# ConvNeXt-V2 block: channel rows on three of every four partitions, every third block stored whole, reloads issued by SP

## The chip, the core and the metric

The kernel runs on one core of one Trainium2 chip. The metric is device time in microseconds (us) of the whole kernel, taken from runs without a profile. One further execution was profiled; the views shown are of that one. TensorE is PE in the profile (its weight loads are PEld), VectorE DVE, ScalarE ACT, GpSimd POOL and SyncE SP.

## The reference

One image `x` of 512 x 512 pixels with 96 channels, bf16:

```python
out = depthwise_conv3x3(x, dw)            # zero padding
h   = layernorm(out, over the 96 channels) # no gain or bias
h   = gelu(h @ w1)                         # 96 -> 384
gx  = sqrt(sum over all pixels of h*h + 1e-6)      # one number for each of 384
nx  = gx / (mean(gx) + 1e-6)
h   = grn_gamma * (h * nx) + grn_beta + h
return x + h @ w2                          # 384 -> 96
```

The sum over all pixels (`gx`) has to be complete before the second matrix product can be finished. So the kernel goes over the image twice.

## The kernel before

The image is cut into 128 blocks of 4 rows (2048 pixels each). `BATCHES` groups them, mostly by four, for the layernorm's statistics.

**First pass.** It is a software pipeline over slots `s`, one block a slot in steady state. The dictionary `at` says which stage of which block is done in which slot. In a slot SP issues, in this order: `load_x` (the block's pixels for four slots later), `stage_read`, `stage_write`, in some slots `stage_bcast` (4 DMAs) or `stage_rows` (2 DMAs), and `store_next` (one third of a stored block). For a block, DVE transposes the pixels, PE does the convolution taps, ACT evacuates (`y_bf`), POOL or ACT squares (`ysq`), PE sums, and POOL multiplies by the inverse deviation (`stage_norm`, tile `yn`). `stage_write` sends `yn` to DRAM (`yn_dram`, 96 channel rows of 4 KB a block, in four DMAs) and one slot later `stage_read` fetches it, channels on partitions, into one of six `ynT` tiles (`yn_ring`). Two slots after that PE multiplies it by the centred `w1p`, and ACT applies the gelu.

A block is four quads of 512 pixels. `cm_quads(b)` says how many quads come out with hidden channels on partitions (DVE then does three `bn_stats` of each); the rest come out with pixels on partitions, and PE sums their squares (`gram_next`). All four quads of a whole block (`is_whole`) are channel-major, and its gelu output goes to `g_dram`: 1.5 MB in three stores. Five late blocks stay in SBUF (`HELD`), and three others keep their `ynT` (`KEPT`).

**Second pass.** `ORDER` mixes blocks that are made again with stored and held ones. Before there are 88 made again (352 quads), 35 whole and 5 held; once the held ones are used up, a stored block follows two or three made ones. For the block at place `n` of `ORDER`:

- `load_rest(n + 5)`: a made block's `ynT` on SP; a stored block's tile `gl` on POOL's queue (two buffers);
- `load_xr(n + 5)`: the block's pixels again (`xr`, five buffers), on POOL's queue;
- `stage_xb(n + 2)`: POOL adds the bias, tile `xb` (three buffers);
- `stage_mm2(n)`: four groups of 12 matmuls (128x96) by `W2s`; after each group DVE adds `xb` and writes `o_sb` (four buffers);
- `stage_out(n - 1)`: SP stores the finished block.

Between the groups `pace` spreads the quads of coming made blocks evenly (`advance`, `recompute`, `cm_unit`): three matmuls of 128x512 on PE, then one ACT gelu of 128x1536. At most three made blocks are held at a time (`GRB`). The first eight places keep program order on every queue (`FIRST`).

The layout of `ynT` before: the 96 channel rows are on partitions 0 to 95, and partitions 96 to 127 meet zero rows of `w1p`. In the second pass `yn_rows` reads 128 rows, that is the block's 96 and the first 32 of the next block, which those zero rows cancel:

```python
    def yn_rows(q):
        return yn_dram[q:q + 2].rearrange("q c (r w) -> (q c) r w", r=GR)[0:128]
...
                if q not in KEPT:
                    sq.dma_start(out=ynt[:], in_=yn_rows(q))
```

Of the kernel before, what the change touches and what calls it, by code (L numbers as in the profile page):

```python
# [12 lines left out]
GR = 4  # L13
# [3 lines left out]
FILL = (6, 15)  # L17
BATCH = 4
NHELD = 5
WHOLE = (0, 3, 7)  # L20
NTAIL = 14
GRB = 3

# [33 lines left out]
def kernel(  # L57
# [11 lines left out]
    f32 = mybir.dt.float32  # L69
    i32 = mybir.dt.int32  # L70
    bf16 = x.dtype
    assert bf16 == mybir.dt.bfloat16

    B, H, W, C = x.shape
    E = w1.shape[1]
    assert B == 1 and dw.shape[0] == 3 and dw.shape[1] == 3
    assert C == 96 and E % 128 == 0 and W == 512
    NI = C // 32
    NCH = E // 128
    NG = W // 128  # L80
    NBLK = H // GR
# [5 lines left out]
    yn_dram = dram.tile([NBLK, C, GR * W], bf16, name="yn_dram")  # L87
    r_dram = dram.tile([NBLK, GR, W], bf16, name="r_dram")

    TAIL0 = NBLK - NTAIL  # L90
# [3 lines left out]
    def is_held(q):  # L94
        return q in HELD

    def is_whole(q):
        return q < TAIL0 and q % 10 in WHOLE

    def cm_quads(q):  # L100
        if is_whole(q) or is_held(q):
            return NQ
        if q > HELD[0]:
            return 1
        return 2 if q >= NBLK - 16 or (q - 1) % 10 in WHOLE else 3

    whole = [q for q in range(NBLK) if is_whole(q)]
    g_dram = dram.tile([len(whole), 128, NQ * NCH * QW], bf16, name="g_dram")

    def chans(i):  # L110
        return slice(i, 64, 2) if i < 2 else slice(64, 96)
# [8 lines left out]
        return flat_ap.rearrange("p (g r m) -> p g r m", r=GR, m=MB)  # L120

    def yn_src(q):
        return yn_dram[q].rearrange("c (r w) -> c r w", r=GR)

    def yn_rows(q):
        return yn_dram[q:q + 2].rearrange("q c (r w) -> (q c) r w", r=GR)[0:128]

    def yn_dst(q, r):
        return yn_dram[q].rearrange("(c i) (r w) -> r c i w", i=NI, r=GR)[r]
# [1 line left out]
    consts = ctx.enter_context(tc.tile_pool(name="consts", bufs=1))  # L131
# [4 lines left out]
    dwx = consts.tile([9, NI, GR, 32], bf16, name="dwx")  # L136
    eye32 = consts.tile([128, 32], bf16, name="eye32")
    rowsel = consts.tile([128, GR], bf16, name="rowsel")
    w1_raw = consts.tile([C, E], bf16, name="w1_raw")
    w1p = consts.tile([128, E], bf16, name="w1p")  # L140
    Wq = consts.tile([128, NI, 3, GR, 32], bf16, name="Wq")
    w2_sb = consts.tile([128, NCH, C], bf16, name="w2_sb")
# [4 lines left out]
    B2bc_f = consts.tile([128, C], f32, name="B2bc_f")  # L147

    NENT = sum(cm_quads(q) for q in range(NBLK - 2))
    NLAST = cm_quads(NBLK - 2) + cm_quads(NBLK - 1)  # L150
    GROUPS = [min(32, NENT - k) for k in range(0, NENT, 32)] + [NLAST]
    NACC = len(GROUPS)
# [9 lines left out]
    W2s = consts.tile([128, NCH, C], bf16, name="W2s")  # L162
    B2c = consts.tile([128, C], f32, name="B2c")
    free = [[q for q in range(NBLK) if is_whole(q)], list(HELD)]
    free = [v for i, q in enumerate(free[0]) for v in (free[1][i:i + 1] + [q])]
    made_q = KEPT + [q for q in range(NBLK) if not is_whole(q) and not is_held(q) and q not in KEPT]
# [17 lines left out]
    with ExitStack() as p1:  # L184
        pe, dve, act, pool, sp = (InOrder(tc, e) for e in (nc.tensor, nc.vector, nc.scalar, nc.gpsimd, nc.sync))
# [3 lines left out]
        def banks(n):  # L189
            if n == 2:  # L190
                return PS[:, 0:2, :]
            ones[0] += 1
            return PS[:, 2 + ones[0] % 2:3 + ones[0] % 2, :]
# [48 lines left out]
        for b in range(min(2, NBLK)):  # L242
# [3 lines left out]
                       in_=zrow[:, None, :NI * GR * 32].to_broadcast([128, 3, NI * GR * 32]), func=ACTF.Identity)  # L246
# [4 lines left out]
        for q in range(GR):  # L251
            dve.tensor_copy(out=eye32[32 * q:32 * q + 32, :], in_=ident_f[32 * q:32 * q + 32, 32 * q:32 * q + 32])

        cen = consts.tile([C, 128], bf16, name="cen")
        xtpool = pc.enter_context(tc.tile_pool(name="xt", side="right", bufs=1))
        ypool = pc.enter_context(tc.tile_pool(name="ybf", side="right", bufs=13))
        ysqpool = pc.enter_context(tc.tile_pool(name="ysq", side="right", bufs=3))
# [25 lines left out]
        def load_rest(n, sq, pq):  # L283
            q = ORDER[n]
            v = grp.setdefault(q, {})
            if is_held(q):
                v["g"] = gs[q]
            elif is_whole(q):
                v["g"] = late.gl.tile([128, NQ, NCH, QW], bf16, name="gl")
                pq.dma_start(out=v["g"][:].rearrange("p t j w -> p (t j w)"), in_=g_dram[whole.index(q)])  # L290
            else:
                ynt = yn_ring[SLOTS[nth_made[q] % NYT]]
                if q not in KEPT:
                    sq.dma_start(out=ynt[:], in_=yn_rows(q))
                v["ynt"] = ynt

        def recompute(q, t):
# [87 lines left out]
        for j in range(GR):  # L385
            pool.memset(rowsel[32 * j:32 * j + 32, j:j + 1], 1.0)
        pool.memset(cen[:], 1.0)
        pool.memset(w1p[C:128, :], 0.0)
        dve.memset(SG, 0.0)
        busy(FILL[0])  # L390
        Ud = banks(2)[:, 0, :NI * 9].rearrange("p (i k) -> p i k", i=NI)
# [4 lines left out]
        for i in range(NI):  # L396
            dve.tensor_tensor(out=Wd[:, i], in0=eye32[:, None, :].to_broadcast([128, 9, 32]),
                              in1=Ud[:, i, :, None].to_broadcast([128, 9, 32]), op=ALU.mult)
# [13 lines left out]
                            pool.tensor_copy(out=o, in_=i_)  # L412

        for i in range(NI):
            act.dma_start(out=w1_raw[i:C:NI, :], in_=w1[chans(i), :])
        act.dma_start(out=w2_sb[:], in_=w2.rearrange("(j p) c -> p j c", p=128))
        with nc.allow_non_contiguous_dma("tiny gamma/beta load"):
            act.dma_start(out=gam_bf[:], in_=grn_gamma.rearrange("(j p) -> p j", p=128))
# [1 line left out]

        def setup_ynt():
            for t in yn_ring:
                pool.memset(t[C:128, :, :].rearrange("p r w -> p (r w)").bitcast(f32), 0.0)

        def setup_mlp():
            Us = banks(1)[:, 0, :]
            w1m, b2_ps = Us[:, :E], Us[:, E:E + C]
            pe.matmul(w1m, lhsT=cen[:], rhs=w1_raw[:], start=True, stop=True)
            for j in range(NCH):
                pe.matmul(b2_ps, lhsT=bet_bf[:, j:j + 1].to_broadcast([128, 128]), rhs=w2_sb[:, j, :],  # L430
                          start=(j == 0), stop=(j == NCH - 1))
            dve.scalar_tensor_tensor(out=w1p[:C, :], in0=w1m[:C], scalar=-1.0 / C, in1=w1_raw[:],
                                     op0=ALU.mult, op1=ALU.add)
            dve.tensor_copy(out=B2bc_f[:], in_=b2_ps)

# [210 lines left out]

        def stage_read(b):
            t = yn_ring[b % NYT]
            sp.dma_start(out=t[:C], in_=yn_src(b))
            ynts[b] = t  # L650

        bsts = {}
# [2 lines left out]
        for q in range(NBLK):  # L655
            if q == NBLK - 2:
                e_ = 32 * (NACC - 1)
            ents[q] = e_
            e_ += cm_quads(q)
# [166 lines left out]
        for s in range(last_slot + 1):  # L826
# [3 lines left out]
            for b in get("read"):  # L830
                stage_read(b)
# [53 lines left out]
            else:  # L885
                b = mlp[0]
# [38 lines left out]
            if s == 0:  # L925
                setup_ynt()
            if s == 3:
                setup_mlp()
# [18 lines left out]
            if s == last_slot:  # L947
                for n in range(PRE):
                    load_rest(n, sp, sp)
# [19 lines left out]
        r = gi[:].bitcast(f32)  # L969
        for it in range(3):  # L970
# [5 lines left out]
            r = rn_[:]  # L976
# [21 lines left out]
    with p2:  # L998
        def out_part(q, o_sb, sub):
            r0 = q * GR  # L1000
            nc.sync.dma_start(
                out=out[0, r0:r0 + GR].rearrange("r w c -> (r w) c").rearrange(
                    "(p g) c -> p g c", g=PXP)[:, sub * GPS:(sub + 1) * GPS],
                in_=o_sb[:, sub * GPS:(sub + 1) * GPS])

        held = None
        FIRST = 8
        for n, q in enumerate(ORDER):
            sq, pq = (sp, pool) if n < FIRST else (nc.sync, nc.gpsimd)
            if n + PRE < NBLK:  # L1010
                load_rest(n + PRE, sq, pq)
                load_xr(n + PRE, pq)
            if 3 <= n + 2 < NBLK:
                stage_xb(ORDER[n + 2], pq, B2c)
            if n == NBLK - 1:
                stage_out(*held)
                held = None
            o_sb = stage_mm2(n, q)
            if held:
                stage_out(*held)  # L1020
            held = (q, o_sb)
# [30 lines left out]
```

## Time and profile before

| | us |
|---|---|
| median of 3 runs | 1481.22 |
| lowest, highest | 1476.22, 1484.95 |
| span of the profiled execution (first to last instruction) | 1480.8 |
| first `o_sb` add, last `o_sb` add (DVE) | 975.5, 1477.4 |
| ACT, PE, POOL, DVE busy | 1414.4, 1391.3, 1300.3, 1182.0 |

The page gives no time of the profiled execution beside its span; the span is 0.4 us below the median and inside the three runs. The first pass takes up to about 970 us, the second the remaining 505 us. The shares of busy time are of both together, so each pass has to be read from its own stretch.

### The profile page before, as it was taken

How to read it: one execution, taken by the hardware profiler on the slowest of the kernel's cores; microseconds unless marked ns; L12 is line 12 of the kernel's file. 1: busy time of each engine (PE TensorE's matmuls, PEld its weight loads, DVE VectorE, ACT ScalarE, POOL GpSimd, SP SyncE). 2: the span in 40 equal slices, each digit the busy share in tenths (PEclk: the TensorE clock that was granted, in tenths of full speed). 3: DMA queues.
4: the chain of work that ended last, by engine and by line, in shares of the span. 5: the costliest groups of instructions: out<-in, count | busy, mean ns of one | idle time of the engine just before them, and what ended most of it. 6: DMA issues, size and time to landing. Idle time of an engine off the chain costs nothing.

```text
span 1480.8 us, 54225 instructions
## 1 busy us (share of the span) xinstructions
PE 1391.3 (94%) x23125; PEld 810.4 (55%) x23125; DVE 1182.0 (80%) x2135; ACT 1414.4 (96%) x1595; POOL 1300.3 (88%) x922
## 2 busy tenths in 40 slices
PE   8888999999999999999999997789999999999998
PEld 3434444444444444444444445467777777776776
DVE  7849989999999999999999987965555555555555
ACT  7888989999999999999999999999999999999997
POOL 3459889998998999998999987569999999999997
PEclk9999999999999999999999999999999999999999
DMA  5568788788888888888888866669999999999997
GB/s 180 179 205 255 241 253 280 228 271 260 260 248 264 258 264 255 276 253 254 263 258 266 263 216 195 195 225 409 366 359 402 417 416 413 419 410 417 411 412 282
DMA packets 167768, 433.08 MB, mean 292 GB/s; under 512 B 31558, under 2 KB 81318, under 8 KB 163046
## 3 DMA queue, kind: packets, MB, share of 16 engines
q1 hardware_dynamic: 151284, 326.04, 66.3%
q0 software_dynamic: 14880, 103.43, 17.6%
q8 instruction: 181, 2.97, 0.8%
q14 instruction: 61, 0.50, 0.1%
q10 hardware_dynamic: 1362, 0.15, 0.1%
HBM read 273.30 MB, written 156.22 MB: 290 GB/s over the span
## 4 chain that ended last, share of the span: by engine, by line
PE 30%; ACT 24%; DMA 19%; POOL 13%; DVE 6%; issue 4%; SPq 4%; POOLq 0%; ACTq 0%; DVEq 0%
PE PS L35 30%; ACT g L35 16%; DMA out_dram<-o_sb 9%; POOL yn L35 6%; ACT y_bf L35 5%; POOL ysq L35 5%; SPq L35 4%; DMA yn_dram<-yn 3%; DVE bst L35 3%; DMA xin<-in_x_dram 2%; DMA rbc<-r_dram 2%; DMA ynT<-yn_dram 1%; DMA g_dram<-g 1%; DVE o_sb L35 1%; ACT xT L35 1%
## 5 line engine op out<-in xcount | busy, mean ns | idle before, releaser
L35 ACT ACTIVATE g<-PS 128x512 bf16<-128x512 f32 (+2 forms) x1062 | 727.7, 864 | 16.5 <-PE PS L35 15.6
L35 DVE BATCH_NORM_STATS2 bst<-g 128x6 f32<-128x512 bf16 x1110 | 671.3, 672 | 35.4 <-ACT g L35 34.5
L35 PE MATMUL PS<-ynT,w1p 128*128 128x512 bf16 x2181 | 609.6, 381 | 23.6 <-ACT g L35 5.4
L35 ACT ACTIVATE gr<-PS 128x1536 bf16<-128x1536 f32 x360 | 498.5, 1459 | 18.8 <-PE PS L35 13.8
L35 POOL TENSOR_TENSOR yn<-y_bf,rbc 128x1536 bf16<-128x1536 bf16 x126 | 391.3, 3108 | 77.3 <-ACT rbc L35 21.9
L35 DVE TENSOR_TENSOR o_sb<-PS,xb 128x384 bf16<-128x384 f32 x512 | 277.3, 556 | 227.0 <-PE PS L35 190.1
L324 POOL TENSOR_TENSOR xb<-xr,B2c 128x1536 f32<-128x1536 bf16 x118 | 368.1, 3133 | 4.3 <-DVE o_sb L35 2.0
L35 PE MATMUL PS<-xT,Wq 64*32 64x511 bf16 (+1 forms) x9198 | 340.5, 389 | 26.2 <-ACT y_bf L35 8.1
L35 POOL TENSOR_TENSOR ysq<-y_bf 128x1536 bf16<-128x1536 bf16 x114 | 313.6, 2752 | 12.8 <-ACT y_bf L35 12.8
L35 PEld LDWEIGHTS <-w1p 128*128 128x128 bf16 x2181 | 171.6, 98 | 222.0 <-issue 133.4
L35 PEld LDWEIGHTS <-gr 128*128 128x128 bf16 x4296 | 212.1, 98 | 68.9 <-issue 12.0
L35 PE MATMUL PS<-W2s,gr 128*128 128x96 bf16 x4224 | 223.5, 206 | 8.2 <-DVE o_sb L35 8.0
L35 PEld LDWEIGHTS <-Wq 64*32 64x32 bf16 x9216 | 111.9, 90 | 193.3 <-issue 145.9
L35 ACT ACTIVATE y_bf<-PS 128x1536 bf16<-128x1536 f32 (+2 forms) x135 | 199.4, 1482 | 17.4 <-PE PS L35 13.3
L35 DVE STREAM_TRANSPOSE xT<-xin 128x576 f32<-128x576 f32 (+1 forms) x256 | 181.4, 748 | 8.1 <-DMA xin<-in_x_dram 8.1
L35 PEld LDWEIGHTS <-g 128*128 128x128 bf16 x1704 | 104.9, 98 | 86.3 <-issue 54.3
L35 PE MATMUL PS<-w1p,ynT 128*128 128x256 bf16 (+2 forms) x822 | 125.8, 273 | 8.0 <-ACT xT L35 3.2
L35 PE MATMUL PS<-g 128*128 128x128 bf16 x1464 | 122.6, 220 | 2.9 <-DVE PS L35 2.6
L35 PEld LDWEIGHTS <-gl 128*128 128x128 bf16 x1680 | 82.8, 98 | 26.8 <-issue 5.0
L35 PE MATMUL PS<-W2s,gl 128*128 128x96 bf16 x1680 | 89.5, 206 | 3.4 <-DVE o_sb L35 3.2
L35 PEld LDWEIGHTS <-ynT 128*128 128x128 bf16 x822 | 64.1, 97 | 31.5 <-issue 13.7
L279 POOL DMA_DIRECT2D xr<-in_x_dram x115 | 63.7, 555 | 14.2 <-POOL xb L324 14.2
(105 smaller groups left out, 576.5 us busy)
## 6 DMA issues: line engine op xcount, KB each, us to landing
xin<-in_x_dram SPq DMA_DIRECT2D x126, 432.0 KB
g_dram<-g SPq DMA_DIRECT2D x105, 512.0 KB
gl<-g_dram POOLq DMA_DIRECT2D x35, 1536.0 KB, 11.3
yn_dram<-yn SPq DMA_DIRECT2D x512, 96.0 KB
ynT<-yn_dram SPq DMA_DIRECT2D x128, 384.0 KB
out_dram<-o_sb SPq DMA_DIRECT2D x127, 384.0 KB
xr<-in_x_dram POOLq DMA_DIRECT2D x123, 384.0 KB, 6.9
ynT<-yn_dram SPq DMA_DIRECT2D x85, 512.0 KB
```

The costliest lines, as they stand in the source:

```text
L35: r = f(*a, **k)
L279: pq.dma_start(out=xr[:], in_=x[0, r0:r0 + GR].rearrange("r w c -> (r w) c").rearrange("(p g) c -> p g c", g=PXP))
L324: pq.tensor_tensor(out=xb[:], in0=grp[q]["xr"][:], in1=bias[:, None, :].to_broadcast([128, PXP, C]), op=ALU.add)
```

## The change

Three things are done.

1. **Rows.** The 96 channel rows lie on partitions 4c, 4c+1 and 4c+2; every fourth partition is zeroed once. `w1_raw` is loaded and `w1p` made in that layout. A read of `ynT`, in either pass, is three DMAs of 32 rows (`read_yn`), 384 KB together. In the second pass 128 rows (512 KB) were read with one DMA before.
2. **Stored blocks.** Every third block below the last 14 is whole: 38, not 35. In the second pass 85 blocks (340 quads) are made again, and after the held blocks the pattern is two made, one stored.
3. **Issue.** The 1.5 MB loads of stored blocks (`gl`) are issued by SP, not by POOL.

```diff
-WHOLE = (0, 3, 7)
+WHOLE = 3
...
-        return q < TAIL0 and q % 10 in WHOLE
+        return q < TAIL0 and q % WHOLE == 0
...
-        return 2 if q >= NBLK - 16 or (q - 1) % 10 in WHOLE else 3
+        return 2 if q >= NBLK - 16 or (q - 1) % WHOLE == 0 else 3
...
     def yn_src(q):
-        return yn_dram[q].rearrange("c (r w) -> c r w", r=GR)
-
-    def yn_rows(q):
-        return yn_dram[q:q + 2].rearrange("q c (r w) -> (q c) r w", r=GR)[0:128]
+        return yn_dram[q].rearrange("(c i) (r w) -> i c r w", i=NI, r=GR)
+
+    def read_yn(eng, t, q):
+        for i in range(NI):
+            eng.dma_start(out=t[i:128:4], in_=yn_src(q)[i])
...
-    w1_raw = consts.tile([C, E], bf16, name="w1_raw")
+    w1_raw = consts.tile([128, E], bf16, name="w1_raw")
...
-        cen = consts.tile([C, 128], bf16, name="cen")
+        cen = consts.tile([128, 128], bf16, name="cen")
...
-                pq.dma_start(out=v["g"][:].rearrange("p t j w -> p (t j w)"), in_=g_dram[whole.index(q)])
+                sq.dma_start(out=v["g"][:].rearrange("p t j w -> p (t j w)"), in_=g_dram[whole.index(q)])
...
-                    sq.dma_start(out=ynt[:], in_=yn_rows(q))
+                    read_yn(sq, ynt, q)
...
-        pool.memset(w1p[C:128, :], 0.0)
+        pool.memset(w1_raw[:], 0.0)
...
-            act.dma_start(out=w1_raw[i:C:NI, :], in_=w1[chans(i), :])
+            act.dma_start(out=w1_raw[i:128:4, :], in_=w1[chans(i), :])
...
-                pool.memset(t[C:128, :, :].rearrange("p r w -> p (r w)").bitcast(f32), 0.0)
+                pool.memset(t[:].rearrange("p r w -> p (r w)").bitcast(f32), 0.0)
...
-            dve.scalar_tensor_tensor(out=w1p[:C, :], in0=w1m[:C], scalar=-1.0 / C, in1=w1_raw[:],
+            dve.scalar_tensor_tensor(out=w1p[:], in0=w1m, scalar=-1.0 / C, in1=w1_raw[:],
...
-            sp.dma_start(out=t[:C], in_=yn_src(b))
+            read_yn(sp, t, b)
```

`NI` is 3, the number of groups of 32 channels.

## The prediction

> **What bounds the kernel now.** I read the busy time by stretches first, since the shares of the whole run mix two passes, then the groups of the second pass, the chain of waits there, and SP's waits in the first pass.
>
> Stretches of the second pass. Columns: stretch, its length, busy us (and instructions) of PE, PEld, DVE, ACT, POOL, then PE clock, DMA share, GB/s:
>
> ```profile
> 1100.00:1200.00 100.00, 98.38 (x1434) 72.86 (x1431) 55.60 (x103) 97.10 (x71) 96.75 (x58) 1.00 1.01 403
> 1200.00:1300.00 100.00, 96.77 (x1417) 71.62 (x1416) 53.87 (x101) 95.23 (x70) 97.04 (x62) 1.00 1.02 416
> 1300.00:1400.00 100.00, 97.06 (x1413) 71.52 (x1410) 54.35 (x101) 95.62 (x70) 95.98 (x58) 1.00 1.02 411
> ```
>
> PE, ACT, POOL and the DMA engines all stand at 95% or more, with only DVE loose. PE, ACT and POOL each leave 2 to 5% idle; the DMA share leaves nothing, at 410 GB/s (mean of the three). So DMA is the first suspect. The waits of 1000 to 1470 us and the chain of 985 to the end say the same:
>
> ```profile
> DVE o_sb L35 <- DMA out_dram<-o_sb: 35.4, 24, 2.7
> PE PS L35 <- DVE o_sb L35: 10.9, 13, 1.6
> ...
> 1205.91 13.80 DMA out_dram<-o_sb
> ```
>
> DVE waits 24 times for an output store to free one of four `o_sb` buffers, and PE then waits for DVE. A store of 384 KB is one microsecond of work at 410 GB/s; it takes 13.8 us because it stands in a full queue.
>
> What each resource needs a block. PE's timeline, and groups of the second pass:
>
> ```profile
> 1200.12 1.18 PE L35 MATMUL PS<-W2s,gl 128*128 128x96 bf16 x24
> 1201.14 0.81 PE L35 MATMUL PS<-ynT,w1p 128*128 128x512 bf16 x3
> 1201.79 0.67 PE L35 MATMUL PS<-W2s,gr 128*128 128x96 bf16 x12
> 1202.30 0.81 PE L35 MATMUL PS<-ynT,w1p 128*128 128x512 bf16 x3
> ...
> 968.51 37.31 ACT L35 ACTIVATE gr<-PS 128x1536 bf16<-128x1536 f32 x27 [1.58 <-PE PS L35]
> ...
> L324 POOL TENSOR_TENSOR xb<-xr,B2c 128x1536 f32<-128x1536 bf16 x118 | 368.1, 3133 | 4.3 <-DVE o_sb L35 2.0 <-POOL xb L324 0.9
> L279 POOL DMA_DIRECT2D xr<-in_x_dram x115 | 63.7, 555 | 14.2 <-POOL xb L324 14.2
> L290 POOL DMA_DIRECT2D gl<-g_dram x33 | 17.7, 536 | 0.2 <-PE PS L35 0.2
> ```
>
> Starts to starts: a quad is 1201.79-1201.14 = 0.65 us of PE, a group of twelve 1202.30-1201.79 = 0.51 us, a gelu 37.31/27 = 1.38 us of ACT. POOL pays 3.13 for `xb`, 0.56 for issuing `xr`, 0.54 for issuing `gl`.
>
> Before, the pattern repeats every 13 places with 9 made and 4 stored blocks, 9/13 x 4 = 2.77 quads a block:
> - PE 2.77 x 0.65 + 4 x 0.51 = 3.84 us
> - ACT 2.77 x 1.38 = 3.82
> - POOL 3.13 + 0.56 + 4/13 x 0.54 = 3.86
> - DMA: `xr` and output 768 KB, 9/13 x 512 and 4/13 x 1536, together 1595 KB = 1.633 MB, at 410 GB/s 3.98
>
> Measured: in 1100 to 1419 us there are 322 adds of `o_sb`, four a block, 319.0 us / (321/4) = 3.975. Only the DMA line meets it. (The rate is measured in the same stretch, so the equality alone is no proof; the share of 1.01 to 1.02 and the stores at 13.8 us are.)
>
> The first pass is ACT's: 757 busy of the 770 us from 150 to 920, DMA share 0.81.
>
> **The change part by part.** *Second pass, bytes.* Now two made, one stored: 768 + 2/3 x 384 + 1/3 x 1536 = 1536 KB = 1.573 MB, at 410 GB/s 3.84 us. PE: 2.67 quads, 1.73 + 2.04 = 3.77. ACT 3.68. POOL 3.69, since the `gl` issues leave it. All four fall, and the latest is still DMA, barely. Gain 3.975 - 3.84 = 0.14 us a block, over the some 101 places behind the last held block: 14 us. In the first 27 places as many blocks are made again as before, the bytes are few, and PE sets the pace: I take 1 us there. Sum -15. The ends: if DMA set the pace everywhere, 198.3 MB go to 190.7 (82 reads of 384 KB for 85 of 512 KB, three more of 1536 KB), -7.6/0.410 = -18.6 us; if PE takes over at once, 12 quads x 0.65 = -7.8 us.
>
> *Twelve gelus fewer* (352 to 340) are 16.6 us of ACT, and 35 `gl` issues 19 us of POOL. Neither is added: both lie beside the DMA.
>
> *Reads in three DMAs.* Does a 128 KB read cost the DMA engines more per byte than a 512 KB one? No row has it. Near rows: `rbc`, also 32 partitions x 4 KB, lies among other DMAs in the first pass. From below, better spreading over the partitions could gain; I take equal. The other end: at 395 GB/s (-3.7%) the whole gain is gone.
>
> On this the Trainium skill speaks against the change: "SBUF — State Buffer", section "Summary: rules for kernel authors", says to use 128 partitions and one DMA rather than several when a transfer is what limits, and gives each transfer a fixed 2 us or so. By it, as an estimate, two more exposed transfers on each of 82 reads would be 328 us. I do not follow it: this trace keeps 403 to 416 GB/s with stores and reads of 384 to 512 KB queued up behind each other, so a fixed latency is covered by the queue.
>
> *SP now issues `gl`.* It waits for the stored block two before, at place n-1, to be through PE. Behind it on SP stand the output store of that same block and the reads; the store needs that block anyway. So it delays nothing new. In the same queue an output store can stand behind a `gl`: 1.573 MB/410 = 3.8 us more. It stood behind it before too, in the same engines by another queue.
>
> *Eight in flight.* By the order of the built kernels, each SP issue also waits for the DMA eight issues before it. Before, 1.7 SP issues a block, so eight spanned 4.7 blocks; now ten issues in three blocks, so eight span 2.4 blocks = 9.2 us. Stores that land in 13.8 us would hold SP up. Yet eight of these, mean 346 KB, are 6.9 us of work left in the engines, so they don't run dry. I take nothing; the other end is in the third rival.
>
> *First pass.* Three more stored blocks are 4.7 MB beside a share of 0.81: covered; nine issues, 4 us of SP spread over 128 slots. Channel-major quads go from 375 to 374; ACT's list is unchanged. The two more issues a read are the point. SP's waits from 150 to 920 us, and its timeline:
>
> ```profile
> SPq L35 <- DMA yn_dram<-yn: 105.7, 118, 3.8
> SPq L35 <- POOL yn L35: 53.9, 32, 4.2
> ...
> 311.61 0.33 SPq L35 DMA_DIRECT2D ynT<-yn_dram  x1
> 312.05 2.49 SPq L35 DMA_DIRECT2D yn_dram<-yn  x4
> 327.90 1.99 SPq L35 DMA_DIRECT2D rbc<-r_dram  x4
> ```
>
> A slot is 7.14 us (108 reads). At `rbc`'s 0.50 us an issue, two more cost 1.0 us a slot. SP's waits for engines, all rows of that view that name no DMA, sum to 139 us, 1.28 a slot: that covers it, with 0.28 to spare. Behind the read wait the four writes of the next block, and behind them POOL's `yn` two slots on. I put 0 on it. If the cover is gone, every 0.1 us is 12.8 us.
>
> *The rest.* The memsets have the same length a partition, `w1p`'s extra rows run beside the others, and matmuls cost by columns: nothing, at start-up at most 1 us either way.
>
> Sum: 1480.8 - 15 = 1465.8 for the profiled execution, which stands 0.4 below the median: **1466**.
>
> **The rivals.**
> 1. *PE becomes the bound.* Its 3.77 against DMA's 3.84 is near. Were the DMA stalls already hidden, only the 12 quads count: -7.8, 1473. For it: PE is 68.6% of the chain there. Against: 35 us of DVE waits for stores.
> 2. *Small reads run the engines worse.* At 395 GB/s nothing is gained: 1481. Against it: 403 and 416 GB/s with mixed sizes.
> 3. *SP becomes the bound of the first pass*, the slower one. Place: SP's loop of read, four writes, wait for them to land. If the three reads go at the writes' 0.62 us, the addition is 3 x 0.62 - 0.38 = 1.48 a slot, 0.20 over the cover, x 128 = +26, with -15 in the second pass 1492. It decides from 1.28 us a slot. For it: 118 waits for landed writes, so SP is often late already.
> 4. That it doesn't do what it says: the order shows 85 and 38 blocks and reads of 32 rows, so I leave this out.
>
> **How the numbers follow.** Forecast (1461 to 1471) 0.70; PE bound 0.14; engines worse 0.08; SP bound 0.08. The range reaches from the all-DMA end, -18.6, less 6 us spread of the runs, to the PE end plus the same: 1456 to 1479; the last two rivals are left out of it. A change of 0.5% (7.4 us) is about what a measurement of this kernel can tell from none. Faster by more: nearly all of the first and two thirds of the second, 0.79. Same: 0.12. Slower: 0.09.
>
> **What would show it.** Right: `ynT` reads of 128 KB, 340 gelus of `gr`, GB/s still near 410, 3.84 us a block, fewer waits of `o_sb` for stores, the first pass ending near 970 us. Rival 1: GB/s below 405 with PE unbroken. Rival 2: DMA share 1.0 at a lower GB/s. Rival 3: the second pass starting 20 us or more late, SP's waits for POOL's `yn` gone. Wrong altogether: PE waiting for `gl` or `ynT` in the second pass.

## The result, and the profile after

The changed kernel takes 1567.61 us (median of 6 runs, 1557.21 to 1576.76) against 1481.83 us for the kernel before on the same chip: a ratio of 1.0597, interval 1.056 to 1.0633. The forecast was 1466. The kernel became 6% slower.

Where the time went is read from the first and the last `o_sb` add, which bound the second pass. The profiled span grew by 82.5 us, from 1480.8 to 1563.3:

| | before | after | |
|---|---|---|---|
| first `o_sb` add | 975.5 | 1039.3 | first pass +63.8 us |
| end of the last `o_sb` add | 1477.9 | 1559.5 | second pass 502.5 to 520.2, +17.7 us |
| slot of the first pass (spacing of POOL's `yn`, blocks 20 to 110) | 7.14 | 7.58 | +0.44 us |
| a block of the second pass (places 32 to 112 of `ORDER`) | 3.980 | 4.179 | +0.20 us |

Stretches of the second pass of the kernel after (stretch, length, busy us and instructions of PE, PEld, DVE, ACT, POOL, then PE clock, DMA share, GB/s):

```profile
1100.00:1200.00 100.00, 97.08 (x1435) 72.33 (x1433) 54.94 (x102) 94.70 (x69) 92.03 (x51) 1.00 0.99 364
1200.00:1300.00 100.00, 89.58 (x1319) 66.65 (x1316) 50.62 (x95) 87.06 (x63) 91.10 (x50) 1.00 1.01 378
1300.00:1400.00 100.00, 88.58 (x1302) 65.44 (x1301) 50.40 (x93) 86.70 (x63) 85.62 (x48) 1.00 0.99 367
```

The share of the DMA engines is still 0.99 to 1.01, at 364 to 378 GB/s where it was 403 to 416; from 1200 us on PE falls below 90%. The waits from 1060 to 1530 us (engine, line, what it waited for: us in total, times, longest) show more standing at the output stores:

```profile
DVE o_sb L35 <- DMA out_dram<-o_sb: 58.2, 25, 3.4
...
PE PS L35 <- DVE o_sb L35: 32.2, 28, 2.3
```

SP's own waits in the first pass (150 to 920 us), its timeline there, and the row of the `ynT` reads (count: shortest/median/longest issue in ns, first and last start):

```profile
SPq L35 <- DMA yn_dram<-yn: 36.1, 74, 2.4
...
SPq L35 <- POOL yn L35: 8.1, 6, 3.4
```

```profile
502.69 1.96 SPq L35 DMA_DIRECT2D ynT<-yn_dram  x3
504.75 2.52 SPq L35 DMA_DIRECT2D yn_dram<-yn  x4
```

```profile
L35 SPq DMA_DIRECT2D ynT<-yn_dram x300: 485/588/1929, 152.6 to 914.3; - x150
```

SP hardly waits for POOL's `yn` any more (8.1 us, 53.9 before): it is late itself. The three reads hold it for 1.96 us, where one took 0.33.

### The profile page after: what moved, and what is told of

It is laid out like the page before. It is cut to its first block, busy times and chain, and to the rows that moved or that the text cites. A ratio compares the mean times of both kernels' runs of the same rounds, so it can differ in the third digit from the quotient of the medians.

```text
span 1563.3 us, 54738 instructions
## 1 busy us (share of the span) xinstructions
PE 1405.1 (90%) x23104; PEld 814.8 (52%) x23104; DVE 1189.9 (76%) x2132; ACT 1410.8 (90%) x1583; POOL 1284.3 (82%) x887
## 4 chain that ended last, share of the span: by engine, by line
DMA 23%; POOL 10%; PE 8%; ACT 4%; SPq 3%; DVE 2%; issue 2%; POOLq 0%; DVEq 0%; ACTq 0%
DMA out_dram<-o_sb 14%; PE PS L35 8%; DMA ynT<-yn_dram 6%; POOL xb L325 4%; ACT g L35 3%; SPq L35 3%; POOL ysq L35 2%; POOL yn L35 2%; DVE o_sb L35 1%; DMA rbc<-r_dram 1%; POOL xr L280 1%; DMA yn_dram<-yn 1%; ACT xT L35 1%; DVE bst L35 1%; POOL nt L35 0%
## 5 line engine op out<-in xcount | busy, mean ns | idle before, releaser
L35 ACT ACTIVATE gr<-PS 128x1536 bf16<-128x1536 f32 x348 | 486.0, 1449 | 53.9 <-PE PS L35 47.5
L35 PE MATMUL PS<-xT,Wq 64*32 64x511 bf16 (+1 forms) x9198 | 349.4, 398 | 18.2 <-ACT y_bf L35 4.9
L35 PEld LDWEIGHTS <-gr 128*128 128x128 bf16 x4152 | 205.2, 98 | 94.7 <-issue 43.9
L35 PE MATMUL PS<-W2s,gr 128*128 128x96 bf16 x4080 | 215.8, 206 | 34.9 <-DVE o_sb L35 34.5
L35 ACT ACTIVATE y_bf<-PS 128x1536 bf16<-128x1536 f32 (+2 forms) x135 | 192.3, 1430 | 18.3 <-PE PS L35 14.0
L35 PEld LDWEIGHTS <-g 128*128 128x128 bf16 x1716 | 107.4, 99 | 85.6 <-issue 53.9
L35 PEld LDWEIGHTS <-gl 128*128 128x128 bf16 x1824 | 89.2, 98 | 24.9 <-issue 1.7
L35 PE MATMUL PS<-rowsel,ysq 128*128 128x4 bf16 x1536 | 56.9, 166 | 48.0 <-POOL ysq L35 47.3
L35 PE MATMUL PS<-W2s,gl 128*128 128x96 bf16 x1824 | 95.8, 206 | 1.1 <-DVE o_sb L35 0.9
```

Of the source, the lines that this page charges most:

```text
L35: r = f(*a, **k)
```

## The experiments

The expectations name theories by letters; each says what its theory holds. The questions were two: what lengthened the slot of the first pass, and what took the second pass's gain.

### The parts of the change alone

**Only the rows** (`e1`): the changed kernel with the old 35 whole blocks and `gl` issued by POOL.

```diff
 # against the changed kernel
-WHOLE = 3
+WHOLE = (0, 3, 7)          # and q % 10 in WHOLE, as before
-                sq.dma_start(out=v["g"]...
+                pq.dma_start(out=v["g"]...
```

> Only the row layout with its three reads a block; 35 stored blocks, their reloads issued by POOL. Theory A (the first pass is lost to SP's issue time, each of the three reads costing about 0.6 us of SP): the second pass starts near 1037 us, as with the whole change. For the second pass, theory B (the reloads on SP's queue slow the DMA engines): it is as fast as the bytes allow, some 11 us shorter than before's 502, GB/s near 400, in all about 1532. Theory C (the reads of rows on every fourth partition slow the engines): the second pass is 515 us or more and the whole near 1560. Rival to A (the denser stores of the third stored block fill the first pass): the second pass starts near 975.

**Only the issue** (`e2`): the kernel before with `sq` for `pq` in the `gl` load.

> Only the reloads of stored blocks moved to SP; rows and 35 stored blocks as before. Theory A: the second pass starts at 975 us as before. Theory B: the rate falls to about 370 GB/s, 1.633 MB a block take 4.4 us, about 40 us more, near 1520; packets of 12 KB take some 550 ns, not 477. Theory C: no slower than before, 1478 to 1483.

**Only the stored blocks** (`e3`): the kernel before with `WHOLE = 3`.

> Only every third block stored whole (38), rows read as 128 by one DMA, reloads on POOL. Theories A, B and C: the first pass ends as before, near 975 us. Second pass: 1.66 MB a block at 410 GB/s are 4.05 us if the DMA engines bound it, 7 us more, 1488; if PE bounds it, 12 quads of 0.65 us fewer, 1473. Rival to A (denser stores): the second pass starts 20 us or more later.

**All but the issue** (`e4`): the changed kernel with `pq` for `sq` in the `gl` load.

> The whole change but for the reloads, which POOL issues as before. Theory A: the second pass starts near 1037 us. Theory B: the second pass is 486 to 490 us long, in all about 1528, GB/s near 410. Theory C: it stays near 525 us, in all about 1565.

| kernel | median us | ratio to before | first pass ends | second pass | us a block |
|---|---|---|---|---|---|
| before (profiled) | | | 975.5 | 502.5 | 3.980 |
| e1, rows | 1538.38 | 1.0424 (1.0379 to 1.0468) | 1033.3 | 497.5 | 3.924 |
| e2, issue | 1485.05 | 1.0032 (1.0013 to 1.0052) | 971.0 | 507.4 | 4.034 |
| e3, stored | 1488.79 | 1.0061 (1.0031 to 1.0091) | 971.8 | 506.3 | 4.038 |
| e4, rows and stored | 1542.93 | 1.0438 (1.0410 to 1.0466) | 1039.3 | 498.7 | 3.966 |
| after, all three | 1567.61 | 1.0597 (1.0560 to 1.0633) | 1039.3 | 520.2 | 4.179 |

The "us a block" is the spacing of DVE's adds in places 32 to 112. The whole loss of the first pass comes with the rows (theory A: 1037 expected, 1033.3 and 1039.3 measured) and not with denser stores (e3). For the second pass neither B nor C came out: e1 was expected at some 491 us or at 515 and more, e4 at 486 to 490 or near 525, and 497.5 and 498.7 were measured; e2 lies above C's 1478 to 1483 and far below B's 1520. In the second pass the stored blocks alone go by bytes: 768 + 2/3 x 512 + 1/3 x 1536 KB = 1.660 MB, at 410 GB/s 4.05 us, and 4.038 were measured, though the whole pass grew by 3.8 us and not by 7. The issue on SP costs 0.3% by itself (507.4 against 502.5 us), but 1.5% (1.0597 against 1.0438; 520.2 against 498.7 us) once a read is three DMAs.

The waits tell what holds the second pass of e4. From 1060 to 1530 us DVE never stands for an output store there; it stands for POOL's `xb`:

```profile
DVE o_sb L35 <- POOL xb L325: 77.6, 73, 4.1
```

POOL itself waits 0.2 us for another engine in that stretch and for no DMA: it is full. It nearly was before, by the rows that the prediction shows. Besides the 3.86 us of its sum, POOL stands idle for 14.2 us ahead of 115 `xr` issues, which the view puts down to its own `xb`, 0.12 us a block; that makes 3.98, which meets the measured 3.975 as well as the DMA line does, and for other engines it stood only 2.2 us in 470. Without `gl` issues POOL stands 0.30 us ahead of nearly every `xr` issue, as here in the kernel after:

```profile
1202.41 0.56 POOL L280 DMA_DIRECT2D xr<-in_x_dram  x1 [0.30 <-POOL xb L325]
1202.99 3.13 POOL L325 TENSOR_TENSOR xb<-xr,B2c 128x1536 f32<-128x1536 bf16 x1
```

From one `xb` to the next it takes 3.95 us before, 3.94 in e1, 3.97 in e3 and e4, 4.01 in e2 and e11 (places 32 to 112; in all of these POOL waits 0.01 us a block or less for others). So in these kernels POOL leaves no way much below 3.95 us a block, and with `gl` on SP none below 4.01.

### What a read of 96 rows does to the DMA engines

**One DMA of 96 rows on partitions 0 to 95** (`e5`), in the second pass of e3:

```diff
-                    sq.dma_start(out=ynt[:], in_=yn_rows(q))
+                    sq.dma_start(out=ynt[:C], in_=yn_src(q))
```

> Every third block stored, reloads on POOL, rows on partitions 0 to 95 as before; only the second pass's read changes, from 128 rows to the block's own 96, still one DMA. It brings the bytes of the whole change (1.573 MB a block for two made and one stored) without more DMAs or a stride. First pass as before, second pass starting near 973 us. If the bytes set the pace at before's 410 GB/s, 3.84 us a block and about 1466 in all. If any read that is not 128 partitions wide runs the engines at the 397 GB/s of the whole change with POOL's reloads, 3.96 us a block and about 1477.

**The same rows in three DMAs of 32 neighbouring partitions** (`e6`), in both passes:

```diff
+    def read_yn(eng, t, q):
+        for i in range(NI):
+            eng.dma_start(out=t[32 * i:32 * i + 32], in_=yn_src(q)[32 * i:32 * i + 32])
...
-                    sq.dma_start(out=ynt[:C], in_=yn_src(q))
+                    read_yn(sq, ynt, q)
...
-            sp.dma_start(out=t[:C], in_=yn_src(b))
+            read_yn(sp, t, b)
```

> As the last one, but each read of either pass is split in three DMAs of 32 neighbouring partitions (128 KB that lie together in DRAM). First pass: if the number of SP's issues is what costs, and such an issue takes the 0.42 us of an rbc load, SP needs 0.9 us more a slot and the second pass starts between 975 and 995; if any 32-row read costs 0.59 us, near 1035, as with the strided rows. Second pass: if the split alone slows the engines, 499 us as with strided rows; if the stride does, 486 to 490.

**The 32 rows of a read together in DRAM** (`e7`): e4 with another row order of `yn_dram`.

```diff
-        return yn_dram[q].rearrange("(c i) (r w) -> i c r w", i=NI, r=GR)
+        return yn_dram[q].rearrange("(i c) (r w) -> i c r w", i=NI, r=GR)
...
-        return yn_dram[q].rearrange("(c i) (r w) -> r c i w", i=NI, r=GR)[r]
+        return yn_dram[q].rearrange("(i c) (r w) -> r c i w", i=NI, r=GR)[r]
```

> The whole change with POOL's reloads, but the channel rows are ordered in DRAM so that each of the three reads takes 32 rows that lie together, not every third; on the chip they still go to every fourth partition. First pass: starts the second near 1037 if SP's issues bound it. Second pass: if the stride in DRAM slows the engines, 486 to 490 us; if the partitions or the split do, 499.

Measured: e5 1508.57 us, ratio 1.0148 (1.0108 to 1.0188), first pass as before (977.5), second 529.8; both expectations for its second pass missed. e6 1571.59, 1.0599 (1.0539 to 1.0659), first pass to 1028.5, near 1035 although the median issue took 0.42 us and not 0.59, second 535.5, far over both expectations. e7 1504.36, 1.0121 (1.0069 to 1.0173), first pass to 999.3 and not near 1037, second 497.9, as expected where the order in DRAM does not matter. A stretch of the second pass, e5 first, then e4:

```profile
1200.00:1300.00 100.00, 90.65 (x1314) 67.04 (x1311) 49.94 (x93) 86.68 (x63) 89.19 (x54) 0.98 1.02 370
```

```profile
1200.00:1300.00 100.00, 96.55 (x1427) 71.58 (x1424) 53.99 (x101) 93.87 (x69) 97.04 (x61) 1.00 1.02 403
```

The share (last column but one) is 1.02 in both, but the two are not held by the same thing. In e5 and e6 DVE stands for output stores (58.7 and 45.2 us in places 32 to 112) and POOL for DVE or PE, so there the DMA engines hold the pass: they move 372 GB/s over these places with 96 rows at partitions 0 to 95 in one DMA and 364 in three. In e4, with the rows spread over three of every four partitions, they move 398, and of the engines only SP's issues wait for them. These 398 are what POOL's pace asked for (1.577 MB in 3.966 us) and so the least that they can do; whether they could keep the 410 of the kernel before with such reads, no run shows. So the spread layout is the better way to read 96 rows, and the bytes that it saves came to nothing because POOL was full. Other transfers do take a little longer (mean of a 6 KB packet of `xr`, 1100 to 1400 us: 241 ns before, 254 to 256 in e1, e4 and e7, 274 in e5, 291 in e6). The row order in DRAM does nothing for the second pass (e7: 497.9 against 498.7).

On the second pass the Trainium skill's "SBUF — State Buffer", section "Summary: rules for kernel authors" (128 partitions, one DMA and not several, where a transfer is the limit), held in its direction for neighbouring partitions: 410 GB/s by the rule, 372 and 364 against it. For the spread reads no run decides it. The fixed cost of some 2 us for each transfer, which the same page gives in its section "The DMA setup-cost knee", is not seen here: two more transfers on each of 82 reads did not add 328 us, and e4's second pass is 7.6 us shorter than e3's with one DMA a read.

### What lengthened the first pass

In the first pass e5 and e6 read the same bytes to the same partitions and differ only by the split of the reads, and the slot goes from 7.14 to 7.575 us: three issues suffice, whatever the layout. The trace gives SP's round, from a block's first read to the next block's: issue of the reads, gap to the first write (in brackets what POOL's `yn` was not ready for), issue of four writes, landing of the last, and from there to the next read. Mean us of blocks 20 to 107, from starts, durations and landings of SP's DMAs:

| kernel | reads | gap (`yn`) | writes | landing | next read | slot |
|---|---|---|---|---|---|---|
| before | 0.45 | 0.51 (0.46) | 2.78 | 2.89 | 0.47 | 7.11 |
| e1 | 1.88 | 0.07 (0.01) | 2.85 | 2.05 | 0.68 | 7.54 |
| e6 | 1.65 | 0.07 | 2.74 | 2.61 | 0.50 | 7.57 |
| after | 1.99 | 0.09 (0.02) | 2.82 | 2.02 | 0.66 | 7.58 |
| e7 | 1.89 | 0.07 | 2.42 | 2.41 | 0.51 | 7.30 |
| e8 | 2.02 | 0.06 | 2.76 | 2.99 | 0.25 | 8.08 |
| e13 | 1.80 | 0.48 (0.00) | 3.02 | 2.01 | 0.69 | 8.01 |
| e15 | 0.37 | 0.08 (0.00) | 3.23 | 2.72 | 0.68 | 7.08 |
| e17 | 0.67 | 0.71 (0.66) | 2.69 | 2.28 | 0.71 | 7.06 |
| e18 | 1.26 | 0.17 (0.11) | 2.88 | 2.21 | 0.59 | 7.10 |

In the kernel before SP has 0.46 us a slot in which it stands for POOL's `yn`; in the changed kernel none. e7 issues as many DMAs as e4, but its writes faster (0.44 us each, 0.60 otherwise), and its slot is 0.26 us shorter (7.34 against 7.60 by the spacing of `yn`). Three attempts to shorten the round by order or by another queue failed:

**The x loads on POOL's queue** (`e8`, from e4) and **write before read** (`e9` in the changed kernel, `e10` in e4, `e12` in the kernel before):

```diff
 # e8
-                sp.dma_start(out=o, in_=i_)
+                (sp if b < 8 else pool).dma_start(out=o, in_=i_)
...
 # e9, e10, e12
-            for b in get("read"):
-                stage_read(b)
             for b in get("write"):
                 stage_write(b)
+            for b in get("read"):
+                stage_read(b)
```

> The whole change with POOL's reloads, and the pixel loads of the first pass issued by POOL from block 8 on: one issue of about 0.45 us a slot, and its wait, taken off SP. Theory A (SP's issues bound the first pass): the slot shrinks from 7.60 to about 7.2 us, where POOL with 0.56 us more comes near to being full, and the second pass starts between 985 and 1010. If something else slows the first pass (the reads landing late, the engines), it still starts near 1037.

> The whole change, with one thing turned round: in a slot SP issues the four writes of the next block before the reads of this one. Theory D (the first pass is bound by a loop on SP: the read waits for the block's writes to land, and the next block's writes stand behind the read; the reads' issue, 2.0 us for three, is a link of it): the landing wait drops out, the slot falls from 7.58 to about 7.15 us, the second pass starts at 985 or before, about 1505 in all with the second pass still 520 us long. Rival (SP is simply full: 13 issues of half a microsecond, in whatever order): the slot stays above 7.45, the second pass starts after 1020.

> The same turn, with POOL issuing the reloads. Theory D: second pass from 985 or before, 499 us long, in all 1475 to 1487. Rival (SP is full): above 1520.

> Before, with the same turn of writes and reads and nothing else. Theory D: its loop had 0.5 us a slot in which SP waited for POOL's yn, so it was not the bound, and the slot stays at 7.1 us; 1475 to 1483. If the loop held even before up in many slots, the slot falls to 7.05 or less and the time by 5 us or more.

Measured: e8 1593.64, ratio 1.0728 (1.0680 to 1.0775), slot 8.07. e9 1580.56, 1.0634 (1.0593 to 1.0675), slot 7.73. e10 1562.82, 1.0512 (1.0487 to 1.0536), slot 7.75. e12 1527.92, 1.0288 (1.0259 to 1.0317), slot 7.49, although nothing was added there. (e12's slot and waits are of a profiled execution of 1539.5 us.) All four lengthened the slot of the kernel that they start from. e8 missed both of its expectations (second pass from 1092.3). Theory D's numbers missed in e9, e10 and e12; the rival's limits held in e9 and e10, but a full SP does not by itself say why the slot grew. In e8 the x issues went out of the time in which SP waits for its writes anyway, and the writes landed later (2.99 us); why later stays open. In e12 the read no longer waits for a landing, but SP now stands at the write (waits of SP, 150 to 920 us):

```profile
SPq L35 <- POOL yn L35: 161.7, 56, 6.7
```

and the read and the store of the batch's deviations (`r_dram`) are queued behind that. From the end of DVE's `rt` to the landing of `rbc` it takes 18.8 us in e12, 15.6 before (medians, 150 to 920 us). That number followed the slot (17.5 in e7, 19.3 after, 20.1 in e9), and suggested theory G: this way over SP is the bound.

**`rbc` and `r_dram` first in the slot**: in the changed kernel (`e13`), in e4 (`e14`), in the kernel before (`e15`), in e1 (`e16`).

```diff
+            for k in get("bcast"):
+                stage_bcast(k)
+            for k in get("rows"):
+                stage_rows(k)
             for b in get("read"):
                 stage_read(b)
             for b in get("write"):
                 stage_write(b)
-            for k in get("bcast"):
-                stage_bcast(k)
-            for k in get("rows"):
-                stage_rows(k)
```

> The changed kernel; in each slot of the first pass SP issues the rbc loads and the r_dram store of a batch ahead of the slot's reads and writes of yn instead of behind them. Theory G (the way of the reciprocal deviations over SP, rt to rbc, is what the extra issues lengthened: 15.6 us before, 19.2 after, and POOL stood 73.5 instead of 30.1 us of 770 ahead of yn, which is 0.44 us a slot, the whole growth of the slot): rt to rbc landed falls below 16 us, POOL stands 30 us or less, the slot comes back to 7.1 to 7.25 us, and the time is 1500 to 1515 us; the second pass stays at 520 us. Theory H (SP's own round is full: 6.4 us of issuing in 7.6, whatever the order): slot 7.5 to 7.6, 1560 to 1575 us. Theory D' (the reads come later and the MLP starves, as when read and write were turned): slot 7.7, 1575 to 1590 us.

> As e13, with the reloads of stored blocks issued by POOL as before. Theory G: slot 7.1 to 7.25, second pass 498 us, 1478 to 1495 us, level with the kernel before. Theory H: 1538 to 1548 us. Theory D': 1550 to 1565 us.

> The kernel before with nothing changed but that order. Theory G: POOL's 30.1 us ahead of yn shrink to 20 or less, and ScalarE, busy for 757 of 770 us there, leaves 10 us at most in the pass: 1472 to 1482 us, slot 7.05 to 7.14. Theory H: SP has a third of its time free, no change: 1479 to 1485 us. Theory D': the read later behind rows and rbc in half of the slots, slot 7.2 to 7.4, 1490 to 1510 us.

> The new rows (three reads for one) alone, the old 35 blocks stored whole, reloads issued by POOL, and the rbc loads and r_dram store first in the slot. Theory G: slot 7.1 to 7.25 and the second pass of e1 (497.5 us against 502.5 before): 1474 to 1490 us, perhaps under the kernel before. Theory H: as e1, 1535 to 1542 us. Theory D': 1545 to 1560 us.

Measured: e13 1607.40, ratio 1.0801 (1.0739 to 1.0864), slot 7.98. e14 1580.01, 1.0611 (1.0555 to 1.0667). e16 1577.51, 1.0590 (1.0536 to 1.0644). e15 1475.92, **0.9919 (0.9886 to 0.9952)**, 0.8% below the kernel before and the one gain of these runs. For e13, e14 and e16 no theory's numbers held. In e15 G's time and slot came true (7.09 us), though POOL's standing ahead of `yn` fell only to 26.0 us and not to 20. G is out as the cause of the loss, since the slots of e13, e14 and e16 grew, and `rt` to `rbc` grew with them (20.9 us in e13): it is a sign of SP's lateness. What happened is in SP's waits and timeline of e13:

```profile
SPq L35 <- DMA xin<-in_x_dram: 47.2, 26, 4.3
```

```profile
505.31 0.44 SPq L35 DMA_DIRECT2D xin<-in_x_dram  x1
505.79 2.12 SPq L35 DMA_DIRECT2D rbc<-r_dram  x4
508.03 1.76 SPq L35 DMA_DIRECT2D ynT<-yn_dram  x3
511.72 3.04 SPq L35 DMA_DIRECT2D yn_dram<-yn  x4
```

The first write is the eighth DMA behind the x load and stands 1.93 us (509.79 to 511.72) until that has landed; over the slots the gap ahead of the writes is 0.48 us in place of 0.09. The slot grew by 0.43 (7.58 to 8.01). A wait put into SP's round shows in the slot nearly one for one. In e15 the same wait is there (43.6 us in 28 waits, 150 to 920 us). Its writes take 3.23 us in place of 2.78, and the 0.46 us of standing for `yn` are gone: the slack took it, it seems, and the slot did not grow. ACT, the first pass's bound before, is busy 762.2 of 770 us (757.0 before), and the second pass starts 7.3 us earlier (968.2).

**The dose**: the changed kernel with one (`e17`) or two (`e18`) of the three reads in the first pass.

```diff
-    def read_yn(eng, t, q):
-        for i in range(NI):
+    def read_yn(eng, t, q, n=NI):
+        for i in range(n):
...
-            read_yn(sp, t, b)
+            read_yn(sp, t, b, 1)        # e18: 2
```

> The changed kernel, in whose first pass only one of the three reads of a block is issued, so that the rows of two thirds of the channels stay what they were (the statistics are wrong by it; the arithmetic done is the same in kind and size). Theory H (SP's own round of three reads, four writes and the landing of the last is the bound): the reads' issue falls from 1.99 to 0.6 us a slot, SP comes to wait for POOL's yn again, and ScalarE's 7.02 us a slot are the floor: slot 7.05 to 7.2, first pass 975 to 990 us, total 1495 to 1515. Rival (something else in the new row layout, PE's clock of 0.975 or the zero rows between, holds the pass): slot 7.4 or more, total 1545 us or more.

> As e17 with two of the three reads (one third of the channels is not read in the first pass). Theory H: reads' issue 1.25 us a slot, the slot between: 7.1 to 7.35 us, total 1500 to 1535. Rival of e17: slot 7.4 or more. If the count of DMAs in flight and not the time of issuing decides, the slot follows the number of DMAs in the same way, so this run tells the two apart only by the gap ahead of the first write.

The rows that are not read stay at the zeros of the start in the first pass, so the output of these two is not the reference's; the work of PE, DVE, ACT and POOL is the same in kind and size.

Measured: e17 1489.63, ratio 1.0082 (1.0043 to 1.0121), slot 7.07 as theory H has it, first pass to 964.1, earlier than its 975 to 990. Its profiled execution took 1478.2 us; were all of the 11 us to the median in the first pass, the slot would be some 7.16. e18 1512.78 (two runs), 1.0235 (1.0140 to 1.0330), slot 7.13, first pass to 983.5, within theory H's numbers. The first pass of e17, of e18 and of the kernel after, in that order (150 to 920 us):

```profile
150.00:920.00 770.00, 733.67 (x13056) 367.35 (x13055) 750.26 (x1287) 765.81 (x1060) 715.99 (x540) 1.00 0.72 224
```

```profile
150.00:920.00 770.00, 723.16 (x13051) 364.91 (x13049) 742.34 (x1273) 759.74 (x1058) 713.52 (x539) 1.00 0.77 242
```

```profile
150.00:920.00 770.00, 703.24 (x12506) 341.37 (x12504) 716.15 (x1218) 720.25 (x1013) 673.70 (x504) 0.97 0.78 248
```

ACT (the fourth busy column) is full with one and two reads and loses 40 us with three. That is the shape of a cover used up: 0.67 and 1.26 us of reading are free, 1.99 are not. Layout, weights and code of the second pass are those of the changed kernel, so these are out as causes. Fewer bytes are not the cause either (e5 and e6 read the same), nor the clock of 0.97 in the third line, since PE is busy for 703 of 770 us there. Nor is it waiting for the DMA eight back: in the kernel after, SP's waits for DMAs other than the landing of its writes sum to 4.1 us of 770, and e7 with e4's count of DMAs has the shorter slot. So theory H stands: SP's own round of reads, writes and landing, some 7.1 us without the third read, became the bound of the first pass. What the runs do not explain is the landing: in e6 1.65 us of reads give the same slot as 1.99 after, because the writes land later there (2.61 us).

### Three reads and `gl` in one queue

**e3 with `gl` issued by SP** (`e11`):

> Every third block stored and its reload on SP, but rows read as before (128 rows, one DMA): six SP issues in three blocks of the second pass, not ten. First pass as before, second from about 973. If the reload on SP costs the same with any read (theory E: the queue itself), the second pass is about 526 us, 20 more than with POOL's reloads (506). If it is the three small reads together with the reload on one queue, SP standing at a read until the reload eight issues before has landed (theory F), it is about 511, 5 us more, as with 35 stored blocks.

Measured: 1489.80, ratio 1.0037 (1.0013 to 1.0061), second pass 508.2 us, near theory F's 511 and 1.9 us longer than e3's. With one DMA a read the issue on SP costs 2 to 5 us (e11 and e2); with three it costs 21.5 us (e4 to after). Two more pairs differ by this issue alone in the second pass: 16.0 us (e10 to e9) and 23.5 (e14 to e13). SP's waits in 1060 to 1500 us, e11 and then after, and the timeline of after:

```profile
SPq L352 <- DMA gl<-g_dram: 4.0, 6, 1.3
```

```profile
SPq L127 <- DMA gl<-g_dram: 139.0, 32, 5.5
```

```profile
1241.15 0.33 SPq L291 DMA_DIRECT2D gl<-g_dram  x1
1241.60 0.49 SPq L353 DMA_DIRECT2D out_dram<-o_sb  x1
1242.13 1.78 SPq L127 DMA_DIRECT2D ynT<-yn_dram  x3
1244.34 0.34 SPq L353 DMA_DIRECT2D out_dram<-o_sb  x1
1244.75 7.01 SPq L127 DMA_DIRECT2D ynT<-yn_dram  x3
1253.25 0.34 SPq L353 DMA_DIRECT2D out_dram<-o_sb  x1
```

L127 is the read in `read_yn`. The third read of the second block is the eighth DMA behind `gl`, and the three take 7.01 us instead of 1.78: SP stands until `gl` has landed, with the next output store behind it. In e11 six issues stand in three blocks, and eight span past the landing.

What follows can be read from the stores (places 32 to 112). From DVE's last add of a block to the issue of its store it takes 0.03 us before and in e11, 0.30 in e4, but 3.53 after (7.35 at most); to the landing 11.3, 11.3, 8.8 and 12.7 us in all. So `o_sb` comes free late after: DVE stands 58.2 us for it where e4 shows no such wait, and POOL stands for DVE, 0.12 us a block on top of its 4.01. The cost varies, for a reason that stays open: the same second pass took 509.5 us in e17 and 513.8 in e9, with POOL hardly standing for DVE, 520.4 in e18 and 522.7 in e13.

## Why the prediction was wrong

- **"First pass ... I put 0 on it"** failed, and is the largest term: 64 us. The price of an issue was taken from `rbc` (0.50 us, two more 1.0); the three reads took 1.99 us for 0.45, 1.54 more. The cover of 1.28 us, "all rows of that view that name no DMA", was 1.10 (1.54 less the 0.44 by which the slot grew): 0.4 of it the standing for `yn`, most of the rest the time to the landing, which shrank from 2.89 to 2.02; why it shrank no run shows. An addition of 0.81 us was covered (e18); the predicted 1.0 was not run.
- **"POOL 3.69, since the `gl` issues leave it. All four fall, and the latest is still DMA"** failed. POOL's sum left out that POOL stands idle between its `xb` and its `xr` issue, 0.12 us a block before and 0.30 once `gl` is issued by SP. Without `gl` POOL needs 4.01 us a block (e2, e11), more than the 3.95 before, so the 14 us could not be had, whatever the bytes. "Only the DMA line meets it" was wrong with it. Of the gain 3.8 us came in e4, which leaves `gl` on POOL (498.7 against 502.5), and 5.0 in e1.
- **"Eight in flight ... I take nothing"** failed. The count was right (ten issues in three blocks), and the engines did not run dry as far as the share tells (0.99 to 1.01). But SP stood 139 us at reads, the output stores were issued 3.53 us late, and the second pass became 21.5 us longer, from 498.7 us in e4 to 520.2. That three reads and `gl` in one queue do it together is shown by e4, e11 and the changed kernel.
- **"Reads in three DMAs ... I take equal"** stays open for the spread rows: 398 GB/s were enough for what POOL asked in e4. Rival 2's sign, a share of 1.0 at a lower GB/s, came true without being its cause. For 96 neighbouring partitions its kind of loss is real (372 and 364 GB/s).
- **Rival 3** named the place and the mechanism of the first pass. Its addition of 1.48 us was right within 0.06; with 0.20 over the cover it got +26 and a chance of 0.08, where the slot grew by 0.44. Its sign came true ("SP's waits for POOL's `yn` gone", the second pass 64 us late).
- Right were the bytes of stored blocks (e3: 4.038 us measured, 4.05 by bytes at 410 GB/s), and that three more stored blocks cost the first pass nothing (e3: 971.8). That "`gl` on SP delays nothing new" nearly held as long as a read is one DMA (e2, e11: 2 to 5 us).

## What to carry to other kernels

Before you split a DMA, write out the round of the queue that issues it (issues, waits, landing, next issue) and price each issue by a row with the same partitions and strides; waits are cover only as far as the round really has standing time, and past it every tenth of a microsecond is paid in each slot. When several resources are within a few per cent, add to each engine's sum the idle time between its own instructions, and see in the waits who really waits for whom: a DMA share of 1.0 alone did not tell, and the bytes saved were worth nothing beside a full POOL. Two changes that cost the second pass little or nothing alone (reads in small pieces, a long load on the same queue) can cost together, since the wait for the eighth DMA back is counted in DMAs and not in bytes.

## What was not expected of the hardware

- SP's time to issue a DMA depends on its shape (medians, 150 to 920 us): 96 rows on neighbouring partitions 0.33 us, 32 neighbouring rows 0.42, 32 rows on every fourth partition 0.59, a `yn` write 0.60, and 0.44 when its rows lie together in DRAM. The Trainium skill's "DMA: Bandwidth & Descriptors", section "Issuing engines are not separate DMA queues", calls the time to initiate a DMA usually small beside the DMA; here three issues of 0.59 us carry 384 KB, which are 0.96 us at 410 GB/s.
- DMA engines that show a share of 1.02 moved 363 GB/s (e6, 1200 to 1300 us) to 417 (e3, the same stretch), with the same blocks and only the reads changed; and in e4 the share was 1.01 to 1.02 while no compute engine waited for a DMA. Such a share tells neither the rate nor the bound.
- POOL stands idle for 0.30 us between the end of an `xb` and the issue of the next `xr` load: for nearly every block in e2, e11 and after, and for some four in ten blocks before. Why not in the others no run shows.
- An issue on SP waits for the landing of the one eight before it: seen at `gl` in the second pass and at the x load in e13 and e15.
